# Feed-forward stage of a fused attention kernel: issue order by due dates instead of fixed ranks

## The chip, the core and the metric

The kernel runs on one core of one Trainium2 chip. The metric is the device time of the launch in microseconds, median over runs. Before the change it is 886.52 us, the median of three runs (885.93, 886.52 and 889.31).

## What is computed

The reference is a hash attention followed by a feed-forward layer with a smooth gate. Buckets of query and key come from the signs of six projections, and only pairs of equal buckets attend to each other.

```python
q_bits = (np.einsum('bhsd,dk->bhsk', q, proj) > 0)
k_bits = (np.einsum('bhsd,dk->bhsk', k, proj) > 0)
mask = q_bucket[:, :, :, None] == k_bucket[:, :, None, :]
scores = np.where(mask, scale * np.matmul(q, k.transpose(0, 1, 3, 2)), -1000000000.0)
attn = softmax(scores)
x = np.matmul(attn, v)
h = x @ w_in
sp = np.maximum(h, 0.0) + np.log1p(np.exp(-np.abs(h)))
out = (h * erf(sp)) @ w_out
```

There are 4 batches of 8 heads, 768 positions and 64 columns per head. The feed-forward layer takes 3072 tokens from 512 columns to 2048 and back to 512. Everything that counts here is 32-bit float.

## The kernel before, in words

The attention goes first, over 16 pairs of heads (`attention()`, L435). It ends at about 312 us of the profiled span. Its order is planned by `arrange()`, and the change leaves that call alone (L1081). The feed-forward layer (`feed_forward()`, L1226) follows, over `NTILE` = 6 tiles of 512 tokens.

Both products of the layer are Strassen products: seven block products in place of eight, paid for with additions. In the second product (out of h and `w_out`) each tile has seven products M1, M2, M4, M6, M7, M5, M3, in this order, each of eight pieces (`project`, L1741; two matmuls in the program, four instructions in the trace, 256 columns each). Some of them read sums of quarters of h: `presum_g` (L1723) makes s1 and s2 and changes two quarters. Three of them read sums of blocks of `w_out`: `presum_w` (L1453) makes these once. VectorE and ScalarE gather the products into the output (`combine`, L1784, with the output's DMA on SyncE's queue).

The first product (h out of x and `w_in`) is done in two ways. For tile 0 it is the plain seven products P1, P2, P6, P5, P7, P3, P4 over four column chunks, 28 products of 1.73 us (`plain`, L1311), and each is read out of its PSUM bank by a copy on ScalarE (`read_plain`, L1329) or an addition on VectorE (`complete`, L1332). From tile 1 on, each P product is itself split by Strassen into seven small ones, Q1 to Q4 in the order Q1, Q2, Q6, Q5, Q7, Q3, Q4 (`small`, L1508; eight instructions of 128 columns each), and each is added to h by `add_small` (L1529). Five tiles have 35 such chains of seven. The weights of a chain (1792 KB) are fetched from DRAM into a ring of two slots that lies over the old `w_in` (`load_wi`, L1488). They were put there, during tile 0, by GpSimd (`presum_inner`, L1384, `keep_inner`, L1398) and SyncE (`keep_outer`, L1401). GpSimd also makes the sums of x for the chains (`presum_xi`, L1491, and `presum_x`).

Between the two products stands the gate, on each half quarter of h: `lead`, `factor` twice, `multiply`, `factor` twice, `multiply`, `saturate`, `gate` (L1644 to L1675). `multiply` and `gate` are on VectorE, the others on ScalarE. The gates of tile t must be done before the M products of tile t can read h. From tile 1 on TensorE runs the P chain of tile t+1 and the M chain of tile t alternately.

At the seam the attention leaves four pieces of work that the feed-forward plan takes over as operations named `late` 0 to 6 (L1084): the divisor of the last pair of heads, its inversion (`invert`, L753), its normalisation (`normalise`, L779) with the store of x, and four sums of `w_in` blocks (`presum_weights`, L798). A check of the norms (`judge`, `decide`) goes along too.

**What sets the order.** The program fixes the order of each engine's instructions; engines run them in that order and wait on semaphores. `feed_forward()` makes a list of operations (`Op`, L83), each with an engine, a cost, a rank, what it reads and writes, and `late`, the time from its end until another engine can go on. `arrange()` (L108) then plays them: it takes the engine whose next operation can start first and gives it, among the operations that can start within a small patience of the first, the one of lowest rank. Ranks are written by hand. Rank class 0 holds the products, their read-outs, `add_small` and `combine`; class 1 holds gates, presums and weights. The order of that play is the order of emission. All engines start at time 0 in it. Costs are constants, for instance 1.8 us for `presum_w`, 1.85 us (tile 0) or 1.3 us for `multiply` and `gate`, 0.4 us for `late` 1, and VectorE and GpSimd are taken as independent.

Of the kernel before, what the change touches and what calls it, by code (L numbers as in the profile page):

```python
# [82 lines left out]
class Op:  # L83
# [13 lines left out]
    far: bool = False  # L97
    near: tuple = ()


TABLE_LOAD = 1.28


PATIENCE = 0.16
LENIENCE = 0.3


def arrange(ops, rooms, patience=0.0):  # L108
# [3 lines left out]
    names = {op.name: op for op in ops}  # L112
    users, missing = {}, {}
# [10 lines left out]
    table = "exp"  # L124
# [22 lines left out]
    while len(order) < len(ops):  # L147
        best = None
        for engine, entries in open_ops.items():
            starts = [(start_of(op, at), op) for op, at in entries]  # L150
            starts = [each for each in starts if each[0] < float("inf")]
            if not starts:
                continue
            first = min(start for start, _ in starts)
            start, op = min(
                (
                    (start, op)
                    for start, op in starts
                    if start <= first + (patience if op.rank[0] == 0 and engine != "PE" else 0.0)
                ),  # L160
                key=lambda each: (each[1].rank, each[0]),
            )
# [12 lines left out]
        open_ops[op.engine] = [each for each in open_ops[op.engine] if each[0] is not op]  # L175
        order.append(op)
        for user in users.get(op.name, ()):
            missing[user.name] -= 1
            if not missing[user.name]:
                open_up(user)  # L180
    return order


@with_exitstack
def kernel(
# [1040 lines left out]
    def feed_forward(pools, check, late):  # L1226
# [27 lines left out]
        def op(name, engine, cost, rank, fn, args, reads=(), writes=(), after=(), **more):  # L1254
# [9 lines left out]
            for x in writes:  # L1264
                wrote[x] = name
                read[x] = set()
            needs.discard(name)
            ops.append(
                Op(name, engine, cost, rank, lambda: fn(*args), after=tuple(sorted(needs, key=str)), **more)
            )  # L1270

        def pe(chain, name, cost, rank, fn, args, **more):
            after = more.pop("after", ())
            if last[chain]:
                after += (last[chain],)
            last[chain] = name
            op(name, "PE", cost, rank, fn, args, after=after, late=0.3, **more)

# [57 lines left out]
        def plain_ops():  # L1336
            for c0 in (0, 2):
                for k, (name, n, q, fn) in enumerate(
# [10 lines left out]
                    for c in (c0, c0 + 1):  # L1349
# [15 lines left out]
                            "ACT" if fn is read_plain else "DVE",  # L1365
                            0.58 if fn is read_plain else 0.69,
                            rank,
# [38 lines left out]
        def inner_ops():  # L1406
            for n, name in enumerate(CHAIN):
# [4 lines left out]
                for k in range(4):  # L1412
                    op(
                        ("inner", name, k),
                        "POOL",
                        1.8,
                        (1, (0.1, 0.2, 0.3, 0.4, 0.7, 0.8, 1.0)[n], k),
# [3 lines left out]
                        writes=rooms[k : k + 1],  # L1421
                        after=(("inner", name, k - 1),),
                    )
                op(
                    ("keep", name),
                    "POOL",
                    0.9,
                    (1, 0, n),
# [3 lines left out]
                    writes=(("wi", name, 0),),  # L1432
                    late=8.0,
                )
                if name in ("P6", "P7", "P5", "P3"):
# [8 lines left out]
                        writes=(("wi", name, 1),),  # L1444
                        late=6.0,
                    )
# [18 lines left out]
        def presum_w_ops():  # L1465
            for k in range(4):
                for fl in range(2):
                    op(
                        ("presum_w", fl, k),
                        "DVE",  # L1470
                        1.8,
                        (1, 0.7 + k / 10, fl),
# [3 lines left out]
                        + (tuple(("wt", 0, n) for n in range(4)) if (k, fl) == (3, 0) else ()),  # L1476
                        after=(("presum_w", fl, k - 1),),
                    )

# [72 lines left out]
        def load_ops(t, i):  # L1552
# [10 lines left out]
                + (tuple(("w", name, n) for name in ("P1", "P2", "P4", "P7")) if n < 2 else ()),  # L1563
                late=9.0,
            )

        def chain_ops(t):
            for i, name in enumerate(CHAIN):
# [5 lines left out]
                    "POOL",  # L1574
                    3.2,
# [3 lines left out]
                    writes=(xkey(t, name), ("inn", n % 3)),  # L1579
                )  # L1580
                for g, q in enumerate(INNER):
# [7 lines left out]
                        ("small", t, i, q),  # L1589
                        0.9,  # L1590
                        rank,
# [10 lines left out]
                        "ACT" if copy else "DVE",  # L1602
                        0.58 if copy else 0.69,
                        rank,
# [5 lines left out]
                if name == "P5":  # L1610
                    for fl in range(2):
# [3 lines left out]
                            "POOL",  # L1615
                            1.0,
                            (0, t + 6 / 7, fl),
# [3 lines left out]
                            writes=part(t, 3, fl),  # L1621
                            late=6.0,
                        )
                        op(
                            ("add_both", t, fl),
                            "DVE",
                            1.25,
                            (0, t + 6 / 7, fl),
                            add_both,
                            (t, fl),  # L1630
                            reads=both,
                            writes=part(t, 1, fl),
                        )

# [50 lines left out]
        def gate_ops(t, q):  # L1685
            for fl in range(2):
                me = (t, q, fl)
                if t == 0 and not again:
# [4 lines left out]
                op(  # L1693
                    ("lead",) + me, "ACT", 1.14, (1, when, 0), lead, me,
                    reads=mine, after=chunks(me), take=("e", me), table="sigmoid",
                )
                previous = ("lead",) + me
                for j in range(len(GATE_S)):
                    key = ("w", (j, me))
                    before = ("lead",) + me  # L1700
                    for k in range(len(GATE_S[j][0])):
                        name = ("factor",) + me + (j, k)
                        op(
                            name, "ACT", 1.14, (1, when, 1 + j), factor, me + (j, k),
                            reads=mine, after=(before,), take=None if k else key, table="sigmoid",
                        )
                        before = name
                    op(
                        ("multiply",) + me + (j,), "DVE", 1.3 if t else 1.85, (1, when, j), multiply, me + (j,),
                        after=(before, previous), free=(key,),  # L1710
                    )
                    previous = ("multiply",) + me + (j,)
                op(
                    ("saturate",) + me, "ACT", 1.1, (1, when, 5), saturate, me,
                    after=(previous,), table="sigmoid",
                )
                op(
                    ("gate",) + me, "DVE", 1.3 if t else 1.85, (1, when, 5), gate, me,
                    writes=mine, after=(("saturate",) + me,), free=(("e", me),),
# [92 lines left out]
        def second_ops(t):  # L1812
# [3 lines left out]
            def presums(k, rank):  # L1816
                for fl in range(2):
# [3 lines left out]
                    if t == 0 and k < 2:  # L1821
# [3 lines left out]
                        "DVE",  # L1825
                        1.25,
                        (1, at + rank + 0.01 * fl, k),
                        presum_g,
                        (t, k, fl),
                        reads=reads,  # L1830
                        writes=writes,
                    )

            def products(o, ks=range(8)):
# [3 lines left out]
                for k in ks:  # L1838
                    fls = (0, 1) if apart else (k // G,)
                    reads = ()  # L1840
                    for fl in fls:
# [12 lines left out]
                        (name, t, k),  # L1854
                        0.87,
                        (0, at + (o + (k + 0.5) / 8) / 7 if t or o > 2 else at + (4 * o + 12 * (k // 4) + k % 4) / 56),
# [6 lines left out]
            def combines(*ks):  # L1863
                for k in ks:
# [4 lines left out]
                    if k == 9:  # L1869
# [4 lines left out]
                        "ACT" if what == "copy" else "DVE",  # L1874
                        0.58 if what == "copy" else 0.42 if t == NTILE - 1 and k > 7 else 0.69,
                        (0, at + (ORDER.index(one) + 1 if one in ORDER else 5) / 7, k),
# [34 lines left out]
        def x_ops(t):  # L1911
# [3 lines left out]
                ("load", t), "SP", 1.2, (1, t - 0.95, 0), load_x, (t,),  # L1915
                writes=keys, late=6.0, after=(("late", 2),),
            )
            for k, (what, reads, into) in enumerate(
# [9 lines left out]
                    "POOL",  # L1928
                    1.75,
# [4 lines left out]
                    writes=(xkey(t, into),),  # L1934
                )

# [5 lines left out]
        else:  # L1942
            if late:
                for k in range(3, 7):
                    name = ("P5", "P6", "P7", "P3")[k - 3]
                    reads = {4: (("w", "P5", 1),), 6: (("w", "P6", 1),)}.get(k, ())
                    op(
                        ("late", k), "DVE", 1.8, (1, 0.2, k), late, (k,),
                        reads=reads, writes=(("w", name, 1),), after=(("late", k - 1) if k > 3 else ("complete", 0, 0),),
# [13 lines left out]
        if late:  # L1963
            for k, (engine, cost, name) in enumerate(
                (("PE", 0.8, "P2"), ("DVE", 0.4, "P6"), ("DVE", 1.0, "P5"))
            ):
# [8 lines left out]
                    late=(8.5, 9.0, 3.0)[k],  # L1975
                    far=k == 1,
# [3 lines left out]
            op(("check", 2), "DVE", 0.6, (2, 2, 0), check[2], (), after=(("check", 1),))  # L1980
        listed = arrange(ops, dict(e=2, w=2), PATIENCE)
        closing = [("M3", NTILE - 1, k) for k in range(8)] + [("combine", NTILE - 1, k) for k in (6, 7, 8, 9)]
# [122 lines left out]
```

## Time and profile before

| what | value |
|---|---|
| median of three runs | 886.52 us |
| the profiled execution's own time | 886.08 us |
| its span, first to last instruction | 884.3 us |
| outside the span | 1.78 us |
| VectorE busy | 741.3 us, 84% |
| ScalarE busy | 604.3 us, 68% |
| GpSimd busy | 235.7 us, 27% |
| granted TensorE clock | 1.00 throughout |

Each engine's instructions stand in a timeline with start, duration, source line, operation, output and inputs with shapes, and a count where equal neighbours are merged. Square brackets give the idle time in front and what ended it. PE is TensorE, DVE VectorE, ACT ScalarE, POOL GpSimd, SP SyncE, and SPq its DMA issues. Three small PE rows may lie over each other by some tenths, because the ends of matmuls are modelled; the distance between starts is the better measure of a product.

### The profile page before, as it was taken

How to read it: one execution, taken by the hardware profiler on the slowest of the kernel's cores; microseconds unless marked ns; L12 is line 12 of the kernel's file. 1: busy time of each engine (PE TensorE's matmuls, PEld its weight loads, DVE VectorE, ACT ScalarE, POOL GpSimd, SP SyncE). 2: the span in 40 equal slices, each digit the busy share in tenths (PEclk: the TensorE clock that was granted, in tenths of full speed). 3: DMA queues.
4: the chain of work that ended last, by engine and by line, in shares of the span. 5: the costliest groups of instructions: out<-in, count | busy, mean ns of one | idle time of the engine just before them, and what ended most of it. 6: DMA issues, size and time to landing. Idle time of an engine off the chain costs nothing.

```text
span 884.3 us, 14566 instructions
## 1 busy us (share of the span) xinstructions
PE 872.2 (99%) x5728; PEld 667.7 (76%) x5728; DVE 741.3 (84%) x878; ACT 604.3 (68%) x807; POOL 235.7 (27%) x287
## 2 busy tenths in 40 slices
PE   9999999999999998999999999999999999999998
PEld 5444444444444476898999999999999999999986
DVE  5999999998999799999987868796879777976671
ACT  6888888878888746974777447834792479266830
POOL 1112111111110079893343313232333141110000
PEclk9999999999999999999999999999999999999999
DMA  9577765666661357565574546653773456444201
GB/s 232 139 198 191 228 189 156 169 177 172 193 179 45 108 204 251 200 254 178 178 204 166 179 154 171 224 170 97 203 254 107 158 161 189 163 167 119 50 13 39
DMA packets 96845, 146.60 MB, mean 166 GB/s; under 512 B 34830, under 2 KB 48190, under 8 KB 95872
## 3 DMA queue, kind: packets, MB, share of 16 engines
q1 hardware_dynamic: 87808, 114.67, 41.9%
q0 software_dynamic: 8512, 30.45, 11.7%
q8 instruction: 47, 0.77, 0.4%
q10 hardware_dynamic: 448, 0.46, 0.2%
q14 instruction: 30, 0.25, 0.1%
HBM read 113.21 MB, written 27.10 MB: 159 GB/s over the span
## 4 chain that ended last, share of the span: by engine, by line
PE 91%; DVE 5%; issue 1%; ACT 1%; DVEq 0%
PE M L1762 31%; PE M L1520 24%; PE st L573 17%; PE av L658 13%; PE M L1317 3%; PE bits L861 1%; PE bits L702 1%; DVE area L646 1%; DVE e L1660 1%; DVE area L811 1%; PE warm L822 0%; ACT e_even L600 0%; PE X L1762 0%; ACT e L1671 0%; DVE x L785 0%
## 5 line engine op out<-in xcount | busy, mean ns | idle before, releaser
L1762 PE MATMUL M<-w_out_sb,h 128*128 128x256 f32 x752 | 184.1, 380 | 0.5 <-issue 0.5
L1543 DVE TENSOR_TENSOR h<-M,h 128x512 f32<-128x512 f32 x190 | 130.1, 686 | 49.8 <-PE M L1520 48.7
L573 PE MATMUL st<-q,k 64*128 64x384 f32 x768 | 155.1, 483 | 0.0
L1520 PEld LDWEIGHTS M<-area,w_in_sb 128*128 128x128 f32 x1120 | 144.9, 192 | 8.1 <-issue 0.8
L1660 DVE SCALAR_TENSOR_TENSOR e<-w,e 128x1024 f32<-128x1024 f32 x96 | 132.8, 1383 | 18.6 <-ACT w L1654 18.4
L1520 PE MATMUL M<-area,w_in_sb 128*128 128x128 f32 x1120 | 146.4, 275 | 0.6 <-issue 0.4
L1762 PEld LDWEIGHTS M<-w_out_sb,h 128*128 128x128 f32 x752 | 133.0, 191 | 13.6 <-issue 0.9
L1646 ACT ACTIVATE e<-h,cq 128x1024 f32<-128x1024 f32 x48 | 54.9, 1143 | 111.5 <-DVE h L1543 96.0
L1654 ACT ACTIVATE w<-h,cq 128x1024 f32<-128x1024 f32 x96 | 109.2, 1138 | 9.0 <-DVE e L1660 9.0
L1520 PEld LDWEIGHTS M<-i,w_in_sb 128*128 128x128 f32 x840 | 109.2, 191 | 6.8 <-DVE h L1543 0.8
L1654 ACT ACTIVATE w<-w,cq 128x1024 f32<-128x1024 f32 x96 | 110.2, 1148 | 2.1
L1520 PE MATMUL M<-i,w_in_sb 128*128 128x128 f32 x840 | 110.4, 275 | 0.5 <-DVE h L1543 0.4
L1762 PE MATMUL M<-wt,area 128*128 128x256 f32 x384 | 94.5, 380 | 2.1 <-DVE area L1733 2.1
L573 PEld LDWEIGHTS st<-q,k 64*128 64x128 f32 x768 | 68.5, 187 | 35.8 <-issue 34.4
L1671 ACT ACTIVATE e<-e 128x1024 f32<-128x1024 f32 x48 | 50.6, 1055 | 58.3 <-DVE e L1660 58.1
L646 DVE TENSOR_TENSOR area<-area 128x1536 f32<-128x1536 f32 (+1 forms) x46 | 79.1, 1720 | 6.9 <-ACT area L600 5.7
L1502 POOL TENSOR_TENSOR i<-area,i 128x128 f32<-128x128 f32 x70 | 45.7, 674 | 116.6 <-PE M L1520 115.4
L1762 PEld LDWEIGHTS M<-wt,area 128*128 128x128 f32 x384 | 67.8, 191 | 8.9 <-ACT w L1654 2.5
L600 ACT ACTIVATE e_even<-st 128x768 f32<-128x768 f32 x96 | 73.9, 819 | 0.4 <-PE st L573 0.3
L1675 DVE TENSOR_TENSOR h<-h,e 128x1024 f32<-128x1024 f32 x48 | 64.1, 1335 | 11.3 <-ACT e L1671 11.3
L600 ACT ACTIVATE area<-st 128x768 f32<-128x768 f32 x90 | 72.7, 810 | 0.3 <-PE st L573 0.3
L658 PE MATMUL av<-e_even,v 128*64 128x385 f32 x384 | 65.7, 490 | 0.0
(150 smaller groups left out, 1176.2 us busy)
## 6 DMA issues: line engine op xcount, KB each, us to landing
w_in_sb<-wi_P SPq DMA_DIRECT2D x35, 1792.0 KB
raw<-in_w_out_dram POOLq DMA_DIRECT2D x16, 512.0 KB, 4.2
raw<-in_w_in_dram POOLq DMA_DIRECT2D x14, 512.0 KB, 5.3
v<-in_v_dram SPq DMA_DIRECT2D x32, 192.0 KB
out_dram<-area SPq DMA_DIRECT2D x23, 256.0 KB
q<-in_qkT_dram SPq DMA_DIRECT2D x30, 192.0 KB
k<-in_qkT_dram SPq DMA_DIRECT2D x30, 192.0 KB
r<-rd SPq DMA_DIRECT2D x30, 192.0 KB
```

Source lines behind the costliest of these rows:

```text
L573: nc.tensor.matmul(out=st[:, ab, 0:HS], lhsT=d["k" + src][rows, keys], rhs=d["q" + src][rows, cols], start=(part == 0), stop=(part == 1),)
L600: nc.scalar.activation(out=e[:, :, 0:HS], in_=st[:, :, 0:HS], func=AF.Exp, scale=scale)
L646: nc.vector.tensor_tensor(out=into, in0=one, in1=two, op=ALU.add)
L658: nc.tensor.matmul(out=d["av", half][rows, 0:w], lhsT=d["v"][:, g * GC + c, rows], rhs=e[:, ab, 0:w], start=(g == 0 and c == 0), stop=(g = ...
L1520: nc.tensor.matmul(out=out_[:, c, :], lhsT=ring[:, W_AT[q], n % 2, c * P : (c + 1) * P], rhs=x, start=(q in ("Q1", "Q2", "Q5") and c == 0) ...
L1543: nc.vector.tensor_tensor(out=out_, in0=bank_, in1=one, op=ALU.add)
L1646: nc.scalar.activation(out=s, in_=unit(t, q, fl), func=AF.Sigmoid, bias=cq[:, 0:1])
L1654: nc.scalar.activation(out=st["q", t, q, fl, j], in_=f, func=func, scale=scale, bias=cq[:, column : column + 1])
L1660: nc.vector.scalar_tensor_tensor(out=s, in0=st.pop(("q", t, q, fl, j)), scalar=GATE_S[j][1], in1=s, op0=ALU.add, op1=ALU.mult,)
L1671: nc.scalar.activation(out=s, in_=s, func=AF.Tanh, scale=GATE_LEAD)
L1675: nc.vector.tensor_tensor(out=h, in0=h, in1=st.pop(("s", t, q, fl)), op=ALU.mult)
L1762: nc.tensor.matmul(out=where[:, sub, :], lhsT=a[:, j // G, j % G, sub * P : (sub + 1) * P], rhs=b[:, j, :], start=first, stop=end, skip_gr ...
```

## The change

`feed_forward()` calls a new planner, `by_need()`, in place of `arrange()`. It goes three times through two steps. `dates()` takes TensorE's products in their present order, lets them run without a gap, and gives each its begin as a due date. Every other operation gets the least, over its users, of the user's date less the user's cost, the time between engines and a margin of 0.3 us. `play()` then simulates all engines: TensorE takes the operation of lowest rank that can start, as before, and every other engine takes the one with the earliest due date. No engine waits while it has something that can start (the patience is gone). While VectorE and GpSimd both run an operation marked `port`, both go at 0.54 of their pace.

The default of `late` becomes 0.3 to 0.4 us for every engine (before, 0.06 us for all but TensorE's 0.3 us). Costs are changed: `add_small` 0.69 to 0.61, `multiply` and `gate` 1.3 or 1.85 to 1.16, `presum_w` and `late` 3 to 6 1.8 to 1.16, `presum_inner` 1.8 to 1.26, `presum_xi` 3.2 to 1.9, `late` 2 from 1.0 to 1.45, `decide` 0.6 to 1.7. DMA operations are marked `far`, so that their landing time holds for users on the same queue. The operations themselves, TensorE's ranks and the buffers stay. The attention is not changed.

```diff
+MARGIN = 0.3
+SHARED = 0.54
+def by_need(ops, rooms):
+    def dates(products):
+        begin, t = {}, 0.0
+        for op in products:
+            begin[op.name] = t
+            t += op.cost
...
+        for op in reversed(sorted_ops):
+            due[op.name] = min(
+                [begin.get(op.name, float("inf"))]
+                + [due[user.name] - away(op, user) - user.cost - MARGIN for user in users.get(op.name, ())]
+            )
+        return due
+    def play(due):
...
+        def place(op):
+            return (op.rank if op.engine == "PE" else (due[op.name], op.rank)), op.name
...
+                starts = [(start_of(op), op) for op in entries]
+                first = max(min(start for start, _ in starts), now)
...
+                op = min((op for start, op in starts if start <= first), key=place)
...
+            both = all(engine in running and running[engine][0].port for engine in ("DVE", "POOL"))
+            pace = {engine: SHARED if both and running[engine][0].port else 1.0 for engine in running}
...
+    order = sorted(ops, key=lambda op: op.rank)
+    for _ in range(3):
+        order = play(dates([op for op in order if op.engine == "PE"]))
+    return order
...
+            more.setdefault("late", dict(PE=0.4, DVE=0.3, ACT=0.3, POOL=0.35, SP=0.3)[engine])
...
-        listed = arrange(ops, dict(e=2, w=2), PATIENCE)
+        listed = by_need(ops, dict(e=2, w=2))
```

More of the change, by code (lines that the diff above doesn't have):

```diff
@@ L1276, in pe @@
             last[chain] = name
-            op(name, "PE", cost, rank, fn, args, after=after, late=0.3, **more)
+            op(name, "PE", cost, rank, fn, args, after=after, **more)
         last = dict(P=None, M=None)
@@ L1602, in chain_ops @@
                         "ACT" if copy else "DVE",
-                        0.58 if copy else 0.69,
+                        0.51 if copy else 0.61,
                         rank,
@@ L1708, in gate_ops @@
                     op(
-                        ("multiply",) + me + (j,), "DVE", 1.3 if t else 1.85, (1, when, j), multiply, me + (j,),
+                        ("multiply",) + me + (j,), "DVE", 1.16, (1, when, j), multiply, me + (j,), port=True,
                         after=(before, previous), free=(key,),
@@ L1717, in gate_ops @@
                 op(
-                    ("gate",) + me, "DVE", 1.3 if t else 1.85, (1, when, 5), gate, me,
+                    ("gate",) + me, "DVE", 1.16, (1, when, 5), gate, me, port=True,
                     writes=mine, after=(("saturate",) + me,), free=(("e", me),),
@@ L1874, in combines @@
                         "ACT" if what == "copy" else "DVE",
-                        0.58 if what == "copy" else 0.42 if t == NTILE - 1 and k > 7 else 0.69,
+                        0.51 if what == "copy" else 0.37 if t == NTILE - 1 and k > 7 else 0.61,
                         (0, at + (ORDER.index(one) + 1 if one in ORDER else 5) / 7, k),
@@ L1934, in x_ops @@
                     writes=(xkey(t, into),),
+                    port=True,
                 )
@@ L1947, in feed_forward @@
                     op(
-                        ("late", k), "DVE", 1.8, (1, 0.2, k), late, (k,),
+                        ("late", k), "DVE", 1.16, (1, 0.2, k), late, (k,), port=True,
                         reads=reads, writes=(("w", name, 1),), after=(("late", k - 1) if k > 3 else ("complete", 0, 0),),
```

123 lines of the change are left out of this document (100 added, 23 removed).

## The prediction

> **What bounds the kernel now.** I read the page first, for the shares of the engines.
>
> ```profile
> span 884.3 us, 14566 instructions
> ## 1 busy us (share of the span) xinstructions
> PE 872.2 (99%) x5728; PEld 667.7 (76%) x5728; DVE 741.3 (84%) x878; ACT 604.3 (68%) x807; POOL 235.7 (27%) x287
> ```
>
> TensorE is busy for 872.2 of 884.3 us. The change leaves its products alone, so all that an order can give lies in the 12.1 us in which it is idle. The view of waits, for TensorE alone, says where those are (us in total, how often, the longest).
>
> ```profile
> PE M L1317 <- DVE h L1334: 2.2, 1, 2.2
> PE M L1762 <- DVE area L1733: 2.1, 1, 2.1
> PE M L1317 <- ACT h L1330: 1.5, 1, 1.5
> PE warm L822 <- DVE ones L241: 1.0, 1, 1.0
> PE M L1520 <- DVE h L1543: 0.6, 2, 0.4
> PE M L1762 <- issue: 0.5, 1, 0.5
> PE M L1520 <- issue: 0.4, 1, 0.4
> ```
>
> The line of `warm` is the start of the attention, which the change does not touch. The other six lines are in the feed-forward part and sum to 7.3 us. The remaining 3.8 us of idleness has no wait by this view: it is the launch's ends, and I leave it as it is. Busy time could still hide a product that runs slowly, so I looked at the chain in the steady stage (start, us, what).
>
> ```profile
> 428.50 0.87 PE M L1762 x4
> 429.37 0.89 PE M L1520 x8
> ```
>
> One M piece takes 0.87 us and one small product 0.89 us, each starting where the one before ended. Waits for `add_small` number two in the whole run. So the steady stage is dense, and 7.3 us, 0.8% of the time, is the ceiling of the gain. What a measurement of this kernel can tell from no change is about 0.5%, or 4.4 us.
>
> **The stalls in place.** TensorE's timeline (start, us, line, tiles, count, idle before):
>
> ```profile
> 312.45 5.45 PE L1317 MATMUL M<-area,w_in_sb 128*128 128x256 f32 x24
> ...
> 336.65 3.72 PE L1317 MATMUL M<-area,w_in_sb 128*128 128x256 f32 x16 [2.23 <-DVE h L1334]
> 340.30 0.28 PE L2002 MATMUL X<-stats,ones 64*1 64x64 f32 x4
> 342.09 3.07 PE L1317 MATMUL M<-area,w_in_sb 128*128 128x256 f32 x13 [1.51 <-ACT h L1330]
> ```
>
> The plain products begin at 312.45. At 334.42 TensorE wants the 13th, the first of P4, whose bank `complete` of P7 must have read; it gets it at 336.65. VectorE's timeline says why.
>
> ```profile
> 312.97 2.95 DVE L785 SCALAR_TENSOR_TENSOR x<-x,ev,r 128x768 f32<-128x768 f32 x2
> 315.84 4.51 DVE L1463 TENSOR_TENSOR w_out_sb<-w_out_sb 128x1024 f32<-128x1024 f32 x2
> 320.27 2.29 DVE L1463 TENSOR_TENSOR wt<-w_out_sb 128x1024 f32<-128x1024 f32 x1
> ...
> 330.26 2.30 DVE L1463 TENSOR_TENSOR wt<-w_out_sb 128x1024 f32<-128x1024 f32 x1
> 332.49 1.23 DVE L756 TENSOR_SCALAR zc<-zc 128x12 f32<-128x12 f32 x1
> 333.76 0.23 DVE L759 RECIPROCAL zc<-zc 128x12 f32<-128x12 f32 x1
> 333.90 2.09 DVE L1660 SCALAR_TENSOR_TENSOR e<-w,e 128x1024 f32<-128x1024 f32 x1
> 335.92 1.27 DVE L1334 TENSOR_TENSOR h<-M,h 128x512 f32<-128x512 f32 x2
> ```
>
> VectorE is still at the attention's normalisation until 315.84, so it starts the feed-forward list 3.4 us behind TensorE. From there it has no gap. In front of the two `complete` stand a `presum_w` (2.30), the inversion (1.23 and 0.23) and a `multiply` (2.09). The plan had expected `complete` to be ready later than all of these.
>
> **Part 1: due dates at the seam.** `complete` of P7 is due before the 13th product. The `presum_w` at 330.26 feeds M6, which first runs at 411.56 (a row below shows it), so its date is some 75 us later and it goes behind. Removed from the front, it brings the first `complete` from 335.92 to 333.62 and its end, with half of 1.27 us, to 334.3, where TensorE arrives at 334.42: the stall would be about nothing. Against that, `play()` lets no engine wait: if another long operation can start just before `complete` is ready, it does, and costs up to its length. The three `presum_w` at the head, 4.51 + 2.29 us, stay there for this reason: VectorE has nothing else until the first `complete` is ready. So the first stall lies between 0 and 2.2 us, and I take 0.5, nearer to the end with one `presum_w` less. What is late next is ScalarE: its copy for the 15th product came 1.51 us late, in a queue whose leads had waited for the same `complete`. It gets an early due date, but it held class 0 already, and an activation that has begun holds it up all the same. Between 0 and 1.51, I take 0.9, nearer to the row as it stands.
>
> **The shared port.** The new planner lets VectorE and GpSimd each go at 0.54 of their pace where they overlap. GpSimd's timeline at this place:
>
> ```profile
> 331.45 2.25 POOL L1396 TENSOR_TENSOR h<-area 128x512 f32<-128x512 f32 x1
> 333.65 1.26 POOL L1396 TENSOR_TENSOR h<-area,h 128x512 f32<-128x512 f32 x1
> ```
>
> For long operations the pace fits: 1.16 / 0.54 = 2.15 us by the planner's own numbers, 2.26 to 2.30 in VectorE's rows. The inversion does not fit. It has 12 elements a partition, its neighbour of the same shape takes 0.23 us, and it took 1.23, ending at 333.72 as GpSimd's operation ended at 333.70. It stood still until GpSimd was done. The plan gives that step 0.35 us and no port, where the rows have 1.46. My sum goes by the rows, so the 1.46 us is in it.
>
> [...]
>
> **Part 2: the start of the chains.** TensorE's timeline, the three further stalls:
>
> ```profile
> 374.73 2.02 PE L1520 MATMUL M<-area,w_in_sb 128*128 128x128 f32 x16 [0.43 <-issue]
> ...
> 383.62 1.16 PE L1520 MATMUL M<-i,w_in_sb 128*128 128x128 f32 x8 [0.40 <-DVE h L1543]
> ...
> 411.56 3.69 PE L1762 MATMUL M<-wt,area 128*128 128x256 f32 x16 [2.12 <-DVE area L1733]
> ```
>
> At 374.73 the first small product of a chain waits for something that is no engine, most likely its weights. They can only be fetched once the plain products have left the ring. The plan now has 8.5 us for that fetch in place of 9.0, and M pieces can stand in front. At 383.62 an `add_small` is late; it comes due early and the plan now gives 0.4 and 0.3 us to the hops around it (0.3 and 0.06 before). Of 0.43 + 0.40 = 0.83 us I keep 0.2, with 0 and 0.83 as ends. SyncE's queue is moved too: output stores go with their `combine`, which now may come later, and `load_wi` must not stand behind them. In the plan it does so only from the time at which the `combine` starts, so I cost that at nothing; without this cover a fetch would be late by the length of one `combine`, about an `add_small`, 0.69 us in the next rows.
>
> **Part 3: the gate before M6.** VectorE in front of the stall at 411.56, and the activation that feeds its gate:
>
> ```profile
> 399.89 1.06 ACT L1671 ACTIVATE e<-e 128x1024 f32<-128x1024 f32 x1 [5.96 <-DVE e L1660]
> ```
>
> ```profile
> 405.15 1.21 DVE L1463 TENSOR_TENSOR wt<-w_out_sb,wt 128x1024 f32<-128x1024 f32 x1
> 406.82 0.69 DVE L1543 TENSOR_TENSOR h<-M,h 128x512 f32<-128x512 f32 x1 [0.46 <-PE M L1520]
> 407.43 1.46 DVE L1675 TENSOR_TENSOR h<-h,e 128x1024 f32<-128x1024 f32 x1
> 408.92 1.36 DVE L1733 TENSOR_TENSOR area<-h,h 128x1024 f32<-128x1024 f32 x1
> 410.20 2.35 DVE L1733 TENSOR_TENSOR area<-area,h 128x1024 f32<-128x1024 f32 x2
> ```
>
> `saturate` ended at 400.95, and its `gate` ran at 407.43, 6.5 us later. Between them lay work with lower rank numbers, the `presum_w` at 405.15 among it, which serves M5, two products after M6. Due dates put the gate first. Moved ahead of that row alone it gains 1.21 us, moved to where it is ready 6.5 us; I take 4.5, nearer to the upper end, since only read-outs of banks are as urgent. TensorE will be here earlier by what parts 1 and 2 save, 3.74 - 1.4 = 2.3 and 0.6 us, so the stall without this part would be 2.12 + 2.9 = 5.0 us. That leaves 0.5; I take 0.6.
>
> **The rest, and the sum.** The steady stage has a further 0.2 us of waits now (0.6 less 0.40). Other orders of VectorE there may cost or save some tenths; I allow 0.4. The last line, 0.5 us of issue on L1762, is before the final product behind the program's branch and stays:
>
> ```profile
> 873.69 3.69 PE L1762 MATMUL M<-w_out_sb,h 128*128 128x256 f32 x16 [0.52 <-issue]
> ```
>
> After the change the stalls are 0.5 + 0.9 + 0.2 + 0.6 + 0.4 + 0.5 = 3.1 us, in place of 7.3. The gain is 4.2 us. The profiled execution took 886.08 us, of which 1.78 lie outside its span, so it becomes 881.9; the median of the runs is 0.44 above that execution, which gives 882.3 us.
>
> **The rivals.**
>
> *All of the seam's stalls go.* VectorE's and ScalarE's work arrives in time at all six places, and 0.5 us at the end with some 0.5 elsewhere is left: 886.5 - 6.3 = 880.2 us. For it: the latencies in the plan are longer than before, so real work is early against it. Against it: VectorE is without a gap from 315.84 to the first stall.
>
> *The seam keeps its stall.* VectorE's list begins 3.4 us behind TensorE's in the chip and level with it in the plan, in the new one as in the old. If the slack in the new list is used up, parts of 3.74 us that go at one place come back at the next, up to the 15th product. Then only parts 2 and 3 save: TensorE arrives 0.6 us earlier at M6, the gate is early enough, and 0.6 + 2.1 less the 0.4 allowed elsewhere gives 2.3 us, 884.2. [...]
>
> *The order is nearly the old one.* Read-outs had the lowest rank class already. If due dates give the same lists but for a few places off the path, the time stays: 886.5.
>
> *Slower: read-outs behind long operations in the steady stage.* Nothing waits for an `add_small` that is about to be ready any more, and a gate whose date is earlier goes first. Three times in each of 35 chains a small product needs the bank that an `add_small` has just read: 105 waits. Between stand two M pieces and a small product, 2 x 0.87 + 0.89 = 2.63 us, and `add_small` takes 0.69. A VectorE operation of 1.21 us in front is hidden; one at 2.30 us beside GpSimd gives 2.30 + 0.69 - 2.63 = 0.36 us a time. It decides the sign from 12 hits (4.2 / 0.36); from 24 the kernel is slower by over 0.5%. At 30 it takes 882.3 + 10.8 = 893.1. Against it: GpSimd is busy for 27% of the span and mostly before 400, and the plan sees this contention.
>
> **How the numbers follow.** My forecast has 0.48, and its spread lies about half on each side of the bound of 4.4 us: 0.24 faster, 0.24 same. All stalls gone has 0.20 (faster), the seam's stall kept 0.14 (same), the old order 0.06 (same), the steady stage 0.12 (slower). That makes 0.44, 0.44 and 0.12. The range goes from 879.9, where nearly all of the 6.8 us that an order can remove is gone, to 889.0, which takes in the cases of no gain and up to 18 hits in the steady stage (882.3 + 6.5). The likeliest case alone spans 881 to 884.
>
> **What would show it.** In the waits of the new profile the lines for `complete` (2.2) and `presum_g` (2.1) should be near 0.5 each and ScalarE's 1.5 below 1. In VectorE's timeline no `presum_w` should stand directly before the `complete` of P7, and the gate before M6 should follow its `saturate` within 2 us. The forecast is wrong if lines for `add_small` number tens, if TensorE's line for L1762 grows by waits for a gate or its sums, or if the first stall keeps its 2 us with other work in front.

## The result, and the profile after

The changed kernel takes 882.22 us (median of five runs, 882.18 to 883.00). The kernel before, measured beside it, took 886.96 (five runs, 885.93 to 890.13). The ratio is 0.994, with a 95% interval of 0.9919 to 0.9962: faster by 0.4 to 0.8%. The forecast was 882.3.

The profiled execution took 882.18 us with a span of 880.3. Here are the waits of TensorE that the view lists for it (us in total, how often, the longest). Line numbers are now higher by about a hundred: L1423 is the plain product, L1436 ScalarE's copy, L1440 `complete`, L1572 `presum_w`, L1768 `factor`, L1774 `multiply`, L1785 `saturate`, L1789 `gate`, L1847 `presum_g`, L1876 the M piece.

```profile
PE M L1423 <- ACT h L1436: 2.2, 2, 1.8
PE M L1876 <- ACT e L1785: 1.2, 1, 1.2
PE warm L927 <- DVE ones L346: 1.0, 1, 1.0
PE M L1876 <- DVE area L1847: 0.5, 1, 0.5
PE M L1423 <- DVE h L1440: 0.4, 1, 0.4
PE M L1876 <- issue: 0.2, 1, 0.2
PE st L678 <- ACT e_even L705: 0.2, 1, 0.2
```

The same in place, from TensorE's timeline:

```profile
334.50 3.72 PE L1423 MATMUL M<-area,w_in_sb 128*128 128x256 f32 x16 [0.36 <-DVE h L1440]
...
340.19 1.99 PE L1423 MATMUL M<-area,w_in_sb 128*128 128x256 f32 x8 [1.76 <-ACT h L1436]
342.66 5.45 PE L1423 MATMUL M<-area,w_in_sb 128*128 128x256 f32 x24 [0.48 <-ACT h L1436]
...
407.79 2.83 PE L1876 MATMUL M<-wt,area 128*128 128x256 f32 x12 [1.16 <-ACT e L1785]
...
413.74 1.13 PE L1876 MATMUL M<-wt,area 128*128 128x256 f32 x4 [0.46 <-DVE area L1847]
```

One name here is misleading. A piece of M6 reads a sum made by `presum_g`, and no `saturate`. The view puts the wait of 1.16 us down to the instruction whose end fits best, and a `saturate` (from 406.76, 1.04 us) happened to end at 407.80. VectorE's row for the sum, at 406.17 in the next fence, ends at 407.65, just before TensorE goes on. So the wait belongs to `presum_g`, and the waits at M6 are 1.16 + 0.46 = 1.62 us in all. VectorE and ScalarE at the seam, and VectorE before M6:

```profile
330.32 1.24 DVE L861 TENSOR_SCALAR zc<-zc 128x12 f32<-128x12 f32 x1
331.60 0.23 DVE L864 RECIPROCAL zc<-zc 128x12 f32<-128x12 f32 x1
331.74 2.10 DVE L1572 TENSOR_TENSOR w_out_sb<-w_out_sb 128x1024 f32<-128x1024 f32 x1
333.77 1.28 DVE L1440 TENSOR_TENSOR h<-M,h 128x512 f32<-128x512 f32 x2
334.97 2.33 DVE L1774 SCALAR_TENSOR_TENSOR e<-w,e 128x1024 f32<-128x1024 f32 x1
...
401.98 1.47 DVE L1789 TENSOR_TENSOR h<-h,e 128x1024 f32<-128x1024 f32 x1
403.56 1.29 DVE L1847 TENSOR_TENSOR area<-h,h 128x1024 f32<-128x1024 f32 x1
404.77 1.48 DVE L1774 SCALAR_TENSOR_TENSOR e<-w,e 128x1024 f32<-128x1024 f32 x1
406.17 1.48 DVE L1847 TENSOR_TENSOR area<-area,h 128x1024 f32<-128x1024 f32 x1
```

```profile
335.08 1.15 ACT L1760 ACTIVATE e<-h,cq 128x1024 f32<-128x1024 f32 x1 [1.79 <-DVE h L1440]
337.33 1.15 ACT L1768 ACTIVATE w<-h,cq 128x1024 f32<-128x1024 f32 x1 [1.10 <-DVE e L1774]
338.51 1.15 ACT L1768 ACTIVATE w<-w,cq 128x1024 f32<-128x1024 f32 x1
339.57 0.56 ACT L1436 COPY h<-M 128x512 f32<-128x512 f32 x1
```

The two `complete` now begin at 333.77 (335.92 before). The `presum_w` that stood in front of them before, of `wt`, did go behind (to 350.38). But another one, of `w_out_sb`, which had been second in VectorE's list, has taken its place at 331.74. The `multiply` went behind as well, to 334.97. ScalarE then pays for that: at 337.33 a `factor` has waited for this `multiply` to free its buffer, and the copy that TensorE needs stands behind two `factor` operations, until 339.57.

| wait of TensorE, us | before | forecast | after |
|---|---|---|---|
| `complete`, 13th plain product | 2.23 | 0.5 | 0.36 |
| ScalarE's copies | 1.51 | 0.9 | 2.24 |
| start of the chains | 0.83 | 0.2 | 0 |
| `presum_g`, M6 | 2.12 | 0.6 | 1.62 |
| steady stage | 0.15 | 0.4 | 0 |
| behind the branch | 0.52 | 0.5 | 0.20 |
| sum | 7.36 | 3.1 | 4.42 |

The waits fell by 2.9 us and the span by 4.0. Of the other 1.1 us, 0.28 is the start of the feed-forward part (312.17 for 312.45), which nothing in the change explains: it varies from 312.17 to 313.19 among all kernels tried here, and the attention is the same in all. The remaining 0.8 us lies in distances between products that no view calls a wait: TensorE's busy time itself fell by 1.0 us, from 872.2 to 871.2. It cannot be put down to the change either. From the first plain product to the start of the last product, less the waits, the eight kernels here whose clock stays at 1.00 take between 556.4 and 557.7 us (557.4 before, 556.7 after), and what makes this difference is not known.

### The profile page after: what moved, and what is told of

Read it like the earlier page. It is cut to its first block, busy times and chain, and to the rows that moved or that the text cites. A ratio compares the mean times of both kernels' runs of the same rounds, so it can differ in the third digit from the quotient of the medians.

```text
span 880.3 us, 14576 instructions
## 1 busy us (share of the span) xinstructions
PE 871.2 (99%) x5728; PEld 668.2 (76%) x5728; DVE 735.2 (84%) x878; ACT 605.2 (69%) x807; POOL 239.3 (27%) x287
## 4 chain that ended last, share of the span: by engine, by line
PE 53%; DVE 0%; issue 0%
PE M L1876 30%; PE M L1630 22%; PE X L1876 0%; DVE area L1847 0%; DVE area L1910 0%
## 5 line engine op out<-in xcount | busy, mean ns | idle before, releaser
L1876 PE MATMUL M<-w_out_sb,h 128*128 128x256 f32 x752 | 184.2, 380 | 0.2 <-issue 0.2
L1876 PEld LDWEIGHTS M<-w_out_sb,h 128*128 128x128 f32 x752 | 133.0, 191 | 13.3 <-issue 0.6
L1774 DVE SCALAR_TENSOR_TENSOR e<-w,e 128x1024 f32<-128x1024 f32 x96 | 130.6, 1360 | 14.6 <-ACT w L1768 13.9
L1768 ACT ACTIVATE w<-h,cq 128x1024 f32<-128x1024 f32 x96 | 109.2, 1137 | 24.6 <-DVE e L1774 24.5
L1768 ACT ACTIVATE w<-w,cq 128x1024 f32<-128x1024 f32 x96 | 110.2, 1148 | 2.1
L1630 PE MATMUL M<-i,w_in_sb 128*128 128x128 f32 x840 | 108.6, 275 | 0.0
L1876 PE MATMUL M<-wt,area 128*128 128x256 f32 x384 | 93.8, 380 | 1.6 <-ACT e L1785 1.2
L1785 ACT ACTIVATE e<-e 128x1024 f32<-128x1024 f32 x48 | 50.3, 1051 | 47.6 <-DVE e L1774 47.5
L1612 POOL TENSOR_TENSOR i<-area,i 128x128 f32<-128x128 f32 x70 | 42.6, 629 | 140.6 <-PE M L1630 139.6
L1876 PEld LDWEIGHTS M<-wt,area 128*128 128x128 f32 x384 | 68.1, 191 | 9.0 <-ACT w L1768 1.5
L678 PE MATMUL st<-both 64*128 64x384 bf16 x384 | 63.1, 323 | 0.2 <-ACT e_even L705 0.2
```

Source lines behind the costliest of these rows:

```text
L678: nc.tensor.matmul(out=st[:, ab, 0:HS], lhsT=d["k" + src][rows, keys], rhs=d["q" + src][rows, cols], start=(part == 0), stop=(part == 1),)
L1612: nc.gpsimd.tensor_tensor(out=out_, in0=one_, in1=two_, op=op_)
L1630: nc.tensor.matmul(out=out_[:, c, :], lhsT=ring[:, W_AT[q], n % 2, c * P : (c + 1) * P], rhs=x, start=(q in ("Q1", "Q2", "Q5") and c == 0) ...
L1768: nc.scalar.activation(out=st["q", t, q, fl, j], in_=f, func=func, scale=scale, bias=cq[:, column : column + 1])
L1774: nc.vector.scalar_tensor_tensor(out=s, in0=st.pop(("q", t, q, fl, j)), scalar=GATE_S[j][1], in1=s, op0=ALU.add, op1=ALU.mult,)
L1785: nc.scalar.activation(out=s, in_=s, func=AF.Tanh, scale=GATE_LEAD)
```

## The experiments

Theory S, with which I went in, says that the gain is the order by due dates at the seam, up to the first M6. Its rivals: D, that it is the better durations, whichever planner gets them; W, that all of the feed-forward part gains a little. Three more were formed on the way: O, that what is left at the seam comes from VectorE's list starting 3.4 us late; N, that it comes from engines that may not wait in the plan; P, that contention left out of the plan is what hurts. Ratios are to the kernel before, measured beside each, with 95% intervals.

**Ranks with the new costs (e1).**

```diff
-        listed = by_need(ops, dict(e=2, w=2))
+        listed = arrange(ops, dict(e=2, w=2), 0.16)
```

> The old planner (ranks, patience 0.16) with the new costs, latencies and DMA landing times. Theory S (the gain is the order by due dates at the seam, up to the first M6): TensorE's waits in the feed-forward part stay at 6 us or more and the time within 1.5 us of 887.0. Theory D (the gain is the better durations, whichever planner uses them): waits near 4.4 us, as in the changed kernel, and 882 to 883 us.

**Dates with the old costs (e2).** `by_need()` put into the kernel before, with all its costs, its latencies and no operation marked `port`.

> The new planner fed with the old costs and latencies and no operation marked as using the shared port. Theory S: waits of 4 to 5 us and 882 to 883.5 us, since dates hardly hang on tenths of a cost. Theory D: waits of 6 to 7 us and 886 to 887 us.

e1 took 906.58 us, ratio 1.0224 (1.021 to 1.0238). e2 took 886.17, ratio 0.9993 (0.9984 to 1.0002). Neither half does anything good by itself. TensorE's largest waits, first in e1, then in e2:

```profile
PE M L1630 <- DVE h L1653: 7.5, 1, 7.5
PE M L1423 <- ACT h L1436: 5.5, 2, 5.2
PE M L1630 <- POOL i L1612: 3.5, 4, 0.9
```

```profile
PE M L1422 <- DVE h L1439: 2.6, 1, 2.6
PE M L1625 <- ACT h L1435: 1.8, 1, 1.8
PE M L1625 <- DVE h L1648: 1.2, 2, 0.9
```

e2 has no wait at M6 any more, but it keeps the one for `complete` (2.6) and adds others. S fails on e2 and D fails on e1.

**Half of each order (e4, e5).** e4 issues in the order of the changed kernel up to the first piece of M6, and from there by ranks; e5 the other way round.

```diff
+        cut = ("M6", 0, 0)
+        one, two = by_need(ops, dict(e=2, w=2)), arrange(ops, dict(e=2, w=2), 0.16)
...
+        first = one[: [each.name for each in one].index(cut)]
+        listed = first + [each for each in two if each not in first]
```

> The order of the changed kernel up to the first piece of M6 of tile 0, and from there the order by ranks (with the new costs). Theory S: 882 to 883 us, waits as in the changed kernel. Theory W (the whole of the feed-forward part gains a little): 884 to 886 us.

> The other way round: the order by ranks (with the new costs) up to the first piece of M6 of tile 0, then the order by dates. Theory S: the time of the old planner with the new costs, 886 to 887 us. Theory W: 883 to 885 us.

They took 900.45 us (1.0156, 1.0143 to 1.017) and 900.91 us (1.0164, 1.015 to 1.0177). e4 does not answer its question. Its largest wait stands just behind the cut:

```profile
420.03 3.76 PE L1630 MATMUL M<-i,w_in_sb 128*128 128x128 f32 x16 [13.30 <-DVE h L1653]
```

The two lists disagree on what has been issued there, and the cut itself costs 13.3 us. e5 is of use in its second half: from 412 us on, by dates, TensorE has no wait at all, where e1 by ranks waits 3.5 us for GpSimd's `presum_xi`, in four waits of 0.9 us. With the old costs ranks had no such waits. So the steady stage can be lost by a plan, but between the kernels before and after it differs by 0.15 us of waits only. W is out.

**Full pace for operations marked `port` in the plan (e3).**

```diff
-SHARED = 0.54
+SHARED = 1.0
```

> The changed kernel with the pace beside GpSimd set to 1.0 in the plan, all else as it is. If the planned contention carries the gain: TensorE's wait for complete goes back to 2 us or more, since the plan takes VectorE for nearly twice as quick where both run, and the time to 884 to 887 us. If it does not: 882 to 883 us with the same waits.

It took 901.28 us, 1.0152 (1.0129 to 1.0174), worse than expected. VectorE's head, and ScalarE's first `lead`:

```profile
320.96 2.17 DVE L1572 TENSOR_TENSOR wt<-w_out_sb,wt 128x1024 f32<-128x1024 f32 x1
323.06 2.28 DVE L1572 TENSOR_TENSOR w_out_sb<-w_out_sb 128x1024 f32<-128x1024 f32 x1
325.38 2.17 DVE L1572 TENSOR_TENSOR wt<-w_out_sb 128x1024 f32<-128x1024 f32 x1
327.47 0.68 DVE L1440 TENSOR_TENSOR h<-M,h 128x512 f32<-128x512 f32 x1
```

```profile
331.65 1.15 ACT L1760 ACTIVATE e<-h,cq 128x1024 f32<-128x1024 f32 x1 [10.52 <-DVE h L1440]
```

The plan took each `presum_w` for 1.16 us and put five of them in front of the first `complete`; on the chip they take 2.2 us each. ScalarE stands at a `lead` for 10.52 us with the copies behind it, and TensorE for 5.23 us, as in e1, whose plan has the same short costs and no port either. In all, TensorE's waits from 312 us on are 16.3 us here, for 4.4 in the changed kernel, and its busy time is 7.4 us longer (878.6 for 871.2; the last section shows what slows it).

**VectorE's late start told to the plan (e6).** Nothing is changed but one time in `play()`:

```diff
-            return max(at[op.name], released.get(ring[-room], float("inf")) if len(ring) >= room else 0.0)
+            return max(
+                at[op.name],
+                3.4 if op.engine == "DVE" else 0.0,
+                released.get(ring[-room], float("inf")) if len(ring) >= room else 0.0,
+            )
```

> The changed kernel, but the plan lets VectorE begin 3.4 us later than the other engines, as the trace shows it. Theory O (TensorE's 2.2 us of waiting for ScalarE's copies and 0.4 for complete come from the 3.4 us by which VectorE's list starts late without the plan's knowledge): these waits fall below 1 us together and the time to 880 to 881.5 us. Theory N (they come from operations that start because no engine is let wait): they stay at 2 us or more, 882 to 883 us.

It took 879.39 us, 0.9906 (0.9887 to 0.9926). All six runs (878.69 to 879.65) lie below all five of the changed kernel (882.18 to 883.00). It beats both kernels, and is below the 880 to 881.5 us that O gave. The wait before M6 fell too, to 0.65 us, which O had not said. All that the view still lists of TensorE's waits:

```profile
PE warm L931 <- DVE ones L350: 1.0, 1, 1.0
PE M L1880 <- DVE area L1851: 0.7, 1, 0.7
PE M L1880 <- issue: 0.2, 1, 0.2
PE st L682 <- ACT e_even L709: 0.2, 1, 0.2
```

VectorE's list shows what the plan did with the 3.4 us:

```profile
316.46 2.29 DVE L1576 TENSOR_TENSOR w_out_sb<-w_out_sb 128x1024 f32<-128x1024 f32 x1
318.85 2.11 DVE L1576 TENSOR_TENSOR wt<-w_out_sb 128x1024 f32<-128x1024 f32 x1
320.89 0.68 DVE L1444 TENSOR_TENSOR h<-M,h 128x512 f32<-128x512 f32 x1
```

Two `presum_w` stand at the head, not three. TensorE's first products begin at 313.07 here, so the list does start 3.4 us late. Theory O holds. N does not hold as the only cause: this plan lets no engine wait either, and the waits at the seam are gone.

**Dates along the rings (e7).** A gate also gets a due date from the `lead` that takes its buffer two places later, by the order of the play before.

```diff
...
+                + [due[user.name] - op.late - user.cost - MARGIN for user in takes.get(op.name, ())]
...
```

> The changed kernel, but the due dates also go back along the two-buffer rings of the gates: a gate gets a date from the lead that takes its buffer two places later. If the wait of 1.6 us before M6 comes from a gate that held its buffer too long, for want of a date, it falls below 0.8 us and the time to 881 to 881.8 us. If it comes from the amount of VectorE work before M6, it stays above 1.2 us and 882.2 us.

Half as expected: M6's wait of 1.62 us is gone altogether, and the time is 882.0 us, 0.9935 (0.9916 to 0.9955), no different from the changed kernel. From the first plain product to the start of the last product it takes 560.1 us in the profile, against 561.1; but its attention ended 1.0 us later, at 313.19. That is a gain in its place that these runs cannot tell from none.

**Let engines wait in the plan (e8).** VectorE and ScalarE stay idle if an operation of earlier date can start within 1 us.

```diff
+        def coming(engine, within):
...
+                    for one, rest in running.values():
+                        if one.name in needs[other.name] and rest + away(one, other) <= within:
+                            yield other
...
                 op = min((op for start, op in starts if start <= first), key=place)
+                if engine in ("DVE", "ACT") and any(
+                    place(other) < place(op) for other in coming(engine, 1.0)
+                ):
+                    continue
```

> The changed kernel, but VectorE and ScalarE wait in the plan up to 1 us for an operation of earlier date that is about to be ready. Theory N: the waits at the seam (0.4 for complete, 2.2 for ScalarE's copies) fall below 1 us, 880.5 to 881.5 us. Rival (VectorE has no time to give away there): they fall a little, but gates come late and TensorE waits 3 us or more before M4 and M6, as the plan itself then has it; 884 to 887 us.

It took 884.75 us, 0.9963 (0.9948 to 0.9978).

```profile
PE M L1434 <- ACT h L1447: 1.9, 2, 1.8
PE M L1887 <- DVE area L1858: 1.3, 1, 1.3
...
PE M L1434 <- DVE h L1451: 0.4, 1, 0.4
```

The waits at the seam hardly move (1.9 and 0.4, for 2.24 and 0.36), and those behind it, for gates, their sums and an `add_small`, come to 2.3 us in place of 1.6. VectorE's rows in front of the two `complete` show why this says little about N:

```profile
332.19 2.10 DVE L1583 TENSOR_TENSOR w_out_sb<-w_out_sb 128x1024 f32<-128x1024 f32 x1
334.21 1.27 DVE L1451 TENSOR_TENSOR h<-M,h 128x512 f32<-128x512 f32 x2
```

The same `presum_w` stands there as in the changed kernel. The edit counts an operation as coming only while what it needs is running. The 0.4 us that the plan puts between the end of a product and its `complete` are not covered, and in them the `presum_w` starts. So e8 does not decide whether letting engines wait would help; against N as the only cause stands e6. Why e8 is slower stays open: its profiled execution took 1.7 us longer than the changed kernel's, with 0.15 us more of waits from 312 us on.

**Ranks with contended costs (e9).** e1 again, with the operations marked `port` at the seam at cost / 0.54.

```diff
+        for each in ops:
+            if each.port and (each.engine == "POOL" or each.name[0] in ("presum_w", "late") or each.name[1] == 0):
+                each.cost /= SHARED
+        listed = arrange(ops, dict(e=2, w=2), 0.16)
```

> The old planner with the new latencies and costs, but the operations on the shared port at the seam (presum_w, late 1 to 6 where marked, GpSimd's sums, the gates of tile 0) costed at their contended time, cost / 0.54. Theory P (what made the old planner with new costs lose 20 us is that it took contended operations for short ones): the 5 us wait for ScalarE's copy goes and the time comes back to 883 to 888 us. Theory R (ranks cannot use these latencies: the gates come too late, as the plan itself leaves TensorE 19 us idle): 893 to 905 us.

It took 896.98 us, 1.0115 (1.0082 to 1.0148). P is right on its one point: the wait for ScalarE's copies falls from 5.5 to 0.4 us, so it was the contention left out that made it. R is right on the time, and the largest wait is now for a `gate`:

```profile
381.09 6.33 PE L1876 MATMUL M<-w_out_sb,h 128*128 128x256 f32 x20 [7.59 <-DVE h L1789]
```

**The late start told to the old planner (e10).** The kernel before, and one argument:

```diff
-def arrange(ops, rooms, patience=0.0):
+def arrange(ops, rooms, patience=0.0, begin=()):
...
-    clock = {op.engine: 0.0 for op in ranked}
+    clock = {op.engine: 0.0 for op in ranked} | dict(begin)
...
-        listed = arrange(ops, dict(e=2, w=2), PATIENCE)
+        listed = arrange(ops, dict(e=2, w=2), PATIENCE, dict(DVE=3.4))
```

> The kernel before, with nothing changed but that its plan lets VectorE begin 3.4 us late. If the late start is a cause by itself, whatever the planner: the waits of 2.2 and 1.5 us at the seam fall below 1.5 us together and the time to 883 to 885 us, with the wait before M6 still there. If only dates can use it: 886 to 887 us.

It took 882.57 us, 0.9941 (0.992 to 0.9962): about what the whole change takes.

```profile
PE M L1762 <- DVE area L1733: 1.7, 2, 0.9
PE M L1520 <- DVE h L1543: 1.2, 1, 1.2
PE M L1317 <- ACT h L1330: 1.0, 1, 1.0
```

The seam's 2.23 + 1.51 us are down to 1.0 and the wait before M6 is still there, 1.7 of 2.1, as expected.

**Half of the late start (e12)**, 1.7 in place of 3.4 in e6.

> The changed kernel with 1.7 us in place of 3.4 us for VectorE's late start. Theory O with a smooth dependence: about half of the wait for ScalarE's copies is left, 1 us, and 880.5 to 881.3 us. If the wait hangs on one place in one list that either changes or not: it is at 2.2 us (882.2) or near 0 (879.5).

It took 881.11 us, 0.9926 (0.9902 to 0.9949), between the changed kernel and e6. The wait for copies is 1.3 us, for 2.24 at 0 and none at 3.4: the smooth dependence that O gave.

**Dates, old costs and the late start (e13)**: e2 with the 3.4 us of e6.

> Dates with the old costs and latencies and VectorE's late start of 3.4 us in the plan. If the late start accounts for the waits at the seam in this version as well: they fall from 5 us to below 1.5 us and the time from 886.2 to 881 to 883 us. If the old costs (1.8 us for operations that take 2.3) are what holds it: 885 us or more.

It took 888.52 us, 1.0011 (0.9995 to 1.0026). The seam is free, 0.3 us for 5 in e2, so the late start accounts for the waits there in this version as well. The time is where the rival had it (885 us or more), but the loss has moved to the weights' DMA:

```profile
PE M L1629 <- DMA w_in_sb<-wi_P: 6.6, 2, 4.4
```

TensorE reaches the chains before their weights have come, and then runs them slowly, at a clock of 0.54 and 0.50 behind the two waits (last section). Why the fetches are late there was not tried. The landing times of DMA are among the values that the new plan has and this one lacks, which may be the cause and is not shown.

## Why the prediction came out right

The number was right and the sum only in part. *Part 1, `complete`*: forecast 0.5, measured 0.36. The size held, the step did not: I had VectorE lose a `presum_w` from the front. One went behind and another came in its place; what made room was the `multiply`. The plan fills a gap with whatever can start, as the prediction said of the head of the list. The planner of the changed kernel, played by itself, starts this `presum_w` at 15.87 us of its own time, when `complete` is ready only at 16.77 and the `multiply` at 17.93. In the trace it starts 19.57 us after the first plain product (331.74 less 312.17), 3.7 us behind the plan. *ScalarE's copies*: forecast 0.9, measured 2.24, worse than before. Here the step failed, that the copy would be late by an activation at most. It stood behind two, the first of which had waited for the displaced `multiply`. What was saved at one place came back at the next: that is the second rival, "the seam keeps its stall", whose cause e6, e10 and e12 show. It had a chance of 0.14 as a case of its own; it came in part, within the forecast case: 2.60 of 3.74 us stayed.

*Part 2* went as forecast, 0 for 0.2. *Part 3, M6*: forecast 0.6, measured 1.62. The `gate` came 5.4 us earlier (401.98 for 407.43), more than the 4.5 I took, and TensorE was ready for M6 2.8 us earlier (406.63 for 409.44), near the 2.9 I took. What failed is the step behind the gate, which I took as unchanged. A `multiply` of 1.48 us at 404.77 now stands between the two sums, so that from the start of the gate to M6 it is 5.81 us, for 4.13 before. e7 takes the wait away with that `multiply` still in its place: a gate held a buffer that a later `lead` needed, and had no date for it. With one, the first `multiply` for the gate before M6 runs 2.7 us earlier, counted from the first plain product (393.37 less 313.19, for 395.01 less 312.17). The steady stage and the branch were 0.7 us better than allowed.

All together the waits gave 2.9 us for 4.2. On the profiled execution, 0.3 us of an earlier start and 0.8 us between products, neither in the sum, nearly made up for it: 882.18 for 881.9. The rest is that the median lies 0.04 us above that execution, where the forecast had put 0.44. That the result came within 0.1 us of the forecast is luck; that waits at the seam and at M6 would fall by some us is not.

The rival for the slower side did not come: the changed kernel has no wait for `add_small` in the steady stage. The inversion stood still beside a GpSimd operation again: it took 1.24 us and ended at 331.56, the GpSimd operation at 331.53. Yet a common pace, wrong for this short step, was good enough to plan with, and leaving it out cost 19 us (e3).

What the change is worth is not due dates as such. Old planner and old costs go well together; that 1.8 us for `presum_w` lies between 1.2 alone and 2.3 beside GpSimd may be why, but no run isolates it. New planner, costs, port and latencies go together too. Each mixture tried was no better than before, or worse (e1, e2, e9); the latencies and landing times were not tried by themselves. And the gain itself, 4.7 us, is nearly matched by one number in the old planner (e10, 4.4 us).

## What to carry to other kernels

A plan of issue order that starts all engines at zero is wrong by the amount that one of them brings along from the stage before (3.4 us here); measure that in the trace at the seam and put it into the plan, before changing the planner. On VectorE, without a gap at this seam, the lag of 3.4 us did not go away: it was handed from the wait for `complete` (2.23 us before, 0.36 after) to the wait for ScalarE's copies (1.51 and 2.24). Costs that are used to fill gaps should be those under contention: in e3 and e1 one short estimate, 1.16 us for operations that took 2.17 to 2.28 us in e3, put five long operations in front of an urgent one.

## What the runs showed of the hardware

In some of the kernels a wait of TensorE cost more than itself: the products behind it ran slowly. Windows of two kernels around a wait (us, busy time of PE, PEld, DVE, ACT and POOL, granted TensorE clock, DMA share, GB/s): e13, the wait of 2.13 us in the first row, and the kernel before, with its wait of 2.23 us.

```profile
363.00:366.00 3.00, 0.87 (x5) 0.47 (x3) 2.83 (x2) 1.91 (x3) 2.84 (x3) 1.00 1.01 315
366.00:369.50 3.50, 3.50 (x17) 3.50 (x18) 0.00 (x0) 0.00 (x0) 3.34 (x6) 0.54 1.02 415
```

```profile
334.40:336.60 2.20, 0.02 (x1) 0.00 (x0) 2.20 (x3) 0.00 (x0) 1.88 (x3) 1.00 0.19 62
336.60:340.00 3.40, 3.35 (x16) 2.96 (x16) 3.40 (x4) 2.72 (x3) 3.08 (x4) 1.00 0.97 323
```

In e13 the clock is 0.54 for the 3.5 us that follow, and 16 small instructions took 3.47 us, in place of 2.02 in the kernel before; in the kernel before the clock stays at 1.00. There are eight waits over 4 us here (in e1, e3, e4, e5, e9 and e13), and slow products or a low clock stand behind each. After 5.23 us in e3, 13.30 in e4 and 4.44 in e13 the clock was 0.50; in e4, 16 small instructions then took 3.76 us in place of 1.95. After 5.23 us in e1, 16 plain instructions took 5.60 us in place of 3.72; after 7.47 us there, 8 small ones took 2.08 in place of 1.05. After 7.59 us in e9, 20 instructions of M products took 6.33 us, where 16 ahead of the wait had taken 3.62. The waits of 5.2 and 5.8 us in e5 lie in stretches with a mean clock of 0.90 (312 to 345 us) and 0.89 (366 to 412 us). The slow variants lose more than their waits, and this fits it: e3 has 11.9 us more of waits than the changed kernel and 7.4 us more of busy time, for the same products.

Of the waits between 2.0 and 2.6 us, three left the clock at 1.00 (2.12 and 2.23 before the change, and 2.6 in e2, with a mean of 1.00 from 312 to 345 us), and three had slow products behind them: 2.13 in e13, at 0.54; 2.03 in e3, with 0.83 over the next 2.3 us and 0.56 over the 3 us after those; 2.40 in e1, where 16 small instructions took 3.68 us in place of 2.02. The two of 2.3 us in e5 lie in one stretch with its wait of 5.8 us, whose mean clock is 0.89. So the length alone does not decide there; what does is not shown.
